# Order of the q and oT low parts, of the first layer norms and of the first head tiles in an adaLN attention and gated FFN block

## The chip, the cores and the metric

The kernel runs on one core of a Trainium2 chip. The metric is the device time of one execution in microseconds (us). The engines are named as the profile names them: PE (matrix engine, with PEld for its weight loads), DVE (vector engine), ACT (scalar engine), POOL (GpSimd) and SP, whose queue issues the DMAs and the transposing DMAs.

## The reference

One block of a transformer with adaptive layer norm, all in float32. The shapes: 2048 rows of 512, 32 heads of 128, attention over the last 512 rows of the key and value caches, a feed-forward width of 1376.

```python
mod = (silu(c) @ w_mod).reshape(1, 6, 1, 512)
sa, ca, ga, sb, cb, gb = (mod[:, i] for i in range(6))
h = layernorm(x) * (1 + ca) + sa
# attention: q = h @ wq, per head over the last W = 512 rows of the caches
scores = q @ k.T * 128 ** -0.5
x = x + ga * ((softmax(scores) @ v) @ wo)
h = layernorm(x) * (1 + cb) + sb
x = x + gb * ((gelu(h @ w_gate) * (h @ w_up)) @ w_down)
```

## The kernel before

Each float32 operand of a large matmul is held as a pair of float16 tiles, a high part (a scaled cast) and a low part (the scaled operand less its high part). A product takes three matmuls: high by high, high by low, low by high. The casts are made on ACT, the low parts on DVE (`scalar_tensor_tensor`) or on POOL (a subtraction).

The attention runs over 128 iterations: 16 groups of two heads; in a group, four groups of 512 queries; for each of these, the two heads in turn. One iteration does q = h @ wq for 512 queries (`q_proj`, 12 matmuls of 128x128 by 512 columns into the one PSUM bank psQ), the scores (`s_mm`, 12, in two halves of 256 queries, each into a pair of banks psS of which there are two), the softmax (`s_max` on DVE, `s_exp` on ACT, `s_low` on POOL and the transposing DMAs), probabilities by v (`pv`, 12, into the one bank psO) and the product with wo (`wo_mm`, 12, two banks psW), which DVE adds to the accumulator `acc` (`wo_add`).

The order is written out by hand. `slot(i)` emits one turn: the scores of iteration i, the product with v of iteration i - 2, the product with wo of i - 3 (its first quarter for i - 2), the q projection of i + 2, and the high and low part of q for i + 1 (`q_high` on ACT, L303; `q_low` on DVE, L306) and of the attention output oT for i - 2 (`o_high` on ACT, L368; `o_low` on DVE, L371). Every engine executes its own instructions in the order in which they were emitted, and waits where an operand or a buffer isn't ready.

In `s_max` (L323, L325) DVE takes the maxima of a half's two score rows in one reduction over 128x1024 and makes the exponent's bias of each in an operation on 128x1. `s_exp` (L334, L337) makes two exponentials with their sums and a cast of both to float16. `s_low` (L342) subtracts on POOL and issues two transposing DMAs.

Everything else is hung between as background work: `at(half, f, ...)` puts a call into a list, and `hooks(half)` in `slot` empties the list at that place. A slot has six such places, in this order: 2i + 0.25 (behind the first half's scores), 2i + 0.5, 2i (the end of the first half), 2i + 1.25 (behind the second half's scores), 2i + 1.5, 2i + 1 (the end of the slot). Calls at one place keep the order in which they were put in.

Background work is, in the first slots, the layer norms of the query groups 1 to 3 (`ln_stats`, `ln_norm`, and `ln1_chunk`, which transposes a chunk on PE and makes the pair hh, hl) and the tiles of v and wo of the first two heads (`h_max`, `h_cross_a` and `h_cross_b` for their common scale over all partitions, `h_scalars`, `h_quick`). Later it is loading, scaling and splitting of the next two heads (`load_raw`, `h_max`, `h_scale` on POOL, L272, `h_split` on ACT and POOL, L277 and L278, `h_turn`), the rest of the modulation (`mod_mul`, L559 and L561), the maxima of the feed-forward weights, and in the last slots the first weights of the feed-forward and the second layer norm of the first 512 rows (`ln2_norm`, `ln2_chunk`, `ln2_high`, `ln2_low`). Raw tiles live in eight buffers; a load waits for the last reader of its buffer.

`ln_norm` on ACT needs a factor (L136, on DVE) for a group of four rows, which it makes when first called; on POOL it takes two operations (L139, L140), on DVE one (L142).

The feed-forward follows the last slot: 44 units of 24 matmuls, the activation, and 12 matmuls with w_down.

Of the kernel before, what the change touches and what calls it, by code (L numbers as in the profile page):

```python
# [11 lines left out]
AF = mybir.ActivationFunctionType  # L12
OP = mybir.AluOpType
# [28 lines left out]
def adaln_block(ctx: ExitStack, tc: tile.TileContext, x, k_cache, v_cache, wq, wo,  # L42
                w_gate, w_up, w_down, c_in, w_mod, out):
    nc = tc.nc
# [6 lines left out]
    base = ctx.enter_context(tc.tile_pool(name="base", bufs=1, side="left"))  # L51
# [7 lines left out]
    def small(pool, cols_, bufs=3, name="sm"):  # L59
        return pool.tile([P, cols_], F32, name=name, tag=name, bufs=bufs)  # L60
# [5 lines left out]
    acc = [base.tile([P, D], F32, name=f"acc{t}", tag=f"acc{t}") for t in range(SQ // P)]  # L66
# [10 lines left out]
    mxs = [base.tile([P, P], F32, name=f"mx{i}", tag=f"mx{i}") for i in range(3)]  # L77
# [36 lines left out]
    MV, RS, LNP, LNF = {}, {}, {}, {}  # L114
# [13 lines left out]

    NMR = {}

    def ln_norm(key, dst, src, j, eng=None):
        rs = RS[key][:, j:j + 1]
        if eng is nc.scalar:
            if key not in NMR:
                NMR[key] = small(base, 4, 2, "nmr")
                nc.vector.scalar_tensor_tensor(NMR[key], MV[key][:, :, 0], -1.0, RS[key], op0=OP.mult, op1=OP.mult)  # L136
            nc.scalar.activation(dst, src, AF.Identity, scale=rs, bias=NMR[key][:, j:j + 1])
        elif eng is nc.gpsimd:
            nc.gpsimd.tensor_scalar(dst, src, MV[key][:, j, 0:1], 1.0, op0=OP.subtract, op1=OP.mult)  # L139
            nc.gpsimd.tensor_scalar(dst, dst, rs, 1.0, op0=OP.mult, op1=OP.mult)  # L140
        else:
            nc.vector.tensor_scalar(dst, src, MV[key][:, j, 0:1], rs, op0=OP.subtract, op1=OP.mult)  # L142
# [35 lines left out]
    RAW = {}  # L178
# [39 lines left out]
    HW, DG, IV, AV, ES, RV = {}, {}, {}, {}, {}, {}  # L218
# [17 lines left out]
    def h_scalars(h, part=None):  # L236
        if h not in ES:
            ES[h] = small(base, 2, 5, "es")
            RV[h] = ES[h][:, 1:2]
        if part in (None, "qk"):  # L240
            nc.vector.scalar_tensor_tensor(ES[h][:, 0:1], IV.pop(("wq", h)), sc1[:, 1:2], IV.pop(("k", h)),
                                           op0=OP.mult, op1=OP.mult)
        if part in (None, "vo"):
            nc.vector.scalar_tensor_tensor(ES[h][:, 1:2], IV.pop(("v", h)), 1.0 / ODOWN, IV.pop(("wo", h)),
                                           op0=OP.mult, op1=OP.mult)
# [4 lines left out]
    def h_tile(kind, h):  # L250
        t = right.tile([P, 2, N], F16, name=kind, tag=kind, bufs=BUFS[kind]) if kind != "k" else \
            right.tile([P, 2, N], F16, name="k16", tag="k16", bufs=2)
        (K16 if kind == "k" else HW)[kind, h] = t
        return t

    def h_turn(kind, h):
        t = K16.pop((kind, h))
        kt = HW[kind, h] = right.tile([P, 2, N], F16, name="kT", tag="kT", bufs=BUFS[kind])
        nc.sync.dma_start_transpose(kt.rearrange("p a (b k) -> p (a b) k", b=4), t.rearrange("p a b -> p (a b)"))

    def h_quick(kind, h):
        raw, a = RAW.pop((kind, h)), AV[kind, h]
        t = h_tile(kind, h)
        nc.scalar.activation(t[:, 0, :], raw, AF.Copy, scale=a)
        nc.vector.scalar_tensor_tensor(t[:, 1, :], raw, a, t[:, 0, :], op0=OP.mult, op1=OP.subtract)  # L265
        if kind == "k":
            h_turn(kind, h)


    def h_scale(kind, h):  # L270
# [3 lines left out]
    def h_split(kind, h):  # L274
        raw = RAW.pop((kind, h))
        t = h_tile(kind, h)
        nc.scalar.activation(t[:, 0, :], raw, AF.Copy)  # L277
        nc.gpsimd.tensor_tensor(t[:, 1, :], raw, t[:, 0, :], op=OP.subtract)  # L278
# [26 lines left out]
    def q_low(it):  # L305
        nc.vector.scalar_tensor_tensor(Q[it][:, 1, :], PSQ.pop(it), QDOWN, Q[it][:, 0, :],  # L306
                                       op0=OP.mult, op1=OP.subtract)
# [94 lines left out]
    def ln1_split(qg, c, full, low):  # L402
        pt = LNP.pop((qg, c))
        f = right.tile([P, N], F32, name="h32", tag="h32", bufs=2)
        a, b = colA[1][:, c:c + 1], colB[1][:, c:c + 1]
        if full is nc.scalar:
            nc.scalar.activation(f, pt, AF.Identity, scale=a, bias=b)
            nc.scalar.activation(hh[qg][:, c, :], f, AF.Copy)
        else:
            nc.scalar.activation(hh[qg][:, c, :], pt, AF.Identity, scale=a, bias=b)  # L410
            nc.vector.tensor_scalar(f, pt, a, b, op0=OP.mult, op1=OP.add)
        low.tensor_tensor(hl[qg][:, c, :], f, hh[qg][:, c, :], op=OP.subtract)  # L412
# [4 lines left out]
    V, S_, Y = nc.vector, nc.scalar, nc.gpsimd  # L417
# [3 lines left out]
    for j in range(4):  # L421
        ln_norm(0, acc[j], acc[j], j, S_)
# [5 lines left out]
    for j in (1, 0):  # L428
# [4 lines left out]
        for f in range(NC):  # L433
            n = 4 * (1 - j) + f
# [8 lines left out]
    later = [(kind, h) for h in range(G) for kind in ("v", "wo")]  # L443
# [16 lines left out]
    nc.vector.tensor_scalar_mul(cols[:, 0:8], cols[:, 0:8], sc1[:, 0:1])  # L460
    h_scale("k", 0)
    ln1_split(0, 0, V, V)
    h_quick("wq", 0)
    ln1_split(0, 1, V, V)
    h_split("k", 0)
    h_turn("k", 0)
# [11 lines left out]
    h_cross_b(second, two[:, 1, :])  # L478
    h_scale("k", 1)
    h_scalars(1, "qk")  # L480
    h_quick("wq", 1)
    h_split("k", 1)
    h_turn("k", 1)
    for j in (2, 3):
# [5 lines left out]
    def at(half, f, *a):  # L490
        bg.setdefault(half, []).append((f, a))

    def hooks(half):
        for f, a in bg.pop(half, []):
            f(*a)
# [7 lines left out]
    for j in range(4):  # L503
        at(0.5, ln_norm, 1, acc[4 + j], acc[4 + j], j)
    for c, (tag, full, low) in enumerate((("psW", V, V), ("psW", S_, Y), ("psO", V, V), ("psW", S_, Y))):
        at(1.5, ln1_chunk, 1, c, tag, full, low)
    for j in range(4):
        at(1, ln_stats, 2, acc[8 + j], j)
    for i, kh in enumerate(later):
        at(1, h_max, kh, mxs[2], i)  # L510
    at(1, h_cross_a, later, mxs[2])
    at(2.25, h_cross_b, later)
    for h in range(G):
        at(2.25, h_scalars, h, "vo")
        at(2 + 2 * h, h_quick, "v", h)
        at(3 + 2 * h, h_quick, "wo", h)
    for j in range(4):
        at(2, ln_norm, 2, acc[8 + j], acc[8 + j], j, S_ if j % 2 else Y)
        at(2 + j // 2, ln_stats, 3, acc[12 + j], j)
        at(4, ln_norm, 3, acc[12 + j], acc[12 + j], j, S_ if j % 2 else Y)  # L520
    for c, (half, full, low) in enumerate(((3.5, V, V), (3.5, S_, Y), (4.25, V, V), (4.25, S_, Y))):
        at(half, ln1_chunk, 2, c, "psW", full, low)
# [4 lines left out]
    for g in range(1, NG):  # L527
        b = 2 * PER * (g - 1)
        for n, (dl, dm, dc, dsp) in enumerate(((-3, 0, 5, 8), (2, 5, 9, 12))):
            h = g * G + n  # L530
# [109 lines left out]
    def slot(i):  # L640
        def when(it, f, *a):
            if 0 <= it < NIT:
                f(it, *a)

        when(i, s_mm, 0)
        hooks(2 * i + 0.25)
        when(i - 3, wo_add, 0)
        when(i + 1, q_high)
        when(i - 3, wo_mm, 1)
        when(i, s_max, 0)  # L650
        hooks(2 * i + 0.5)
        when(i, s_exp, 0)
        when(i + 1, q_low)
        when(i, s_low, 0)
        when(i - 2, pv, 0, 2)
        when(i - 3, wo_mm, 2)
        when(i - 3, wo_add, 1)
        when(i - 2, pv, 2, 4)
        hooks(2 * i)

        when(i, s_mm, 1)
        hooks(2 * i + 1.25)
        when(i - 2, o_high)
        when(i - 3, wo_add, 2)
        when(i, s_max, 1)
        hooks(2 * i + 1.5)
        when(i + 2, q_proj, 0, 2)
        when(i, s_exp, 1)
        when(i - 2, o_low)
        when(i, s_low, 1)  # L670
        when(i - 3, wo_mm, 3)
        when(i + 2, q_proj, 2, 4)
        when(i - 2, wo_mm, 0)
        when(i - 3, wo_add, 3)
        when(i - 2, s_rec)
        hooks(2 * i + 1)
# [172 lines left out]
    for j in range(4):  # L849
        at(e + 4, x1_load, 0, j)  # L850
        n = e + 8 + (j + 1) // 2
# [4 lines left out]
    for f in range(NDA):  # L856
        at(e + 6, wd_load, f)
        at(e + 11 + f, ff_scale, "d", f)
        at(e + 12 + f, ff_part, "d", f)
    for c, (a, b) in enumerate(((13.5, 13), (13, 14.5), (14.5, 14), (14, 15.5))):  # L860
        at(e + a, ln2_chunk, 0, c, nc.vector if c % 2 else nc.scalar)
        at(e + a, ln2_high, 0, c)
        at(e + b, ln2_low, 0, c, nc.gpsimd)
# [10 lines left out]
    for i in range(NIT + 3):  # L874
        slot(i)
# [3 lines left out]
    while nd < NU:  # L879
# [5 lines left out]
        if u < NU:  # L885
# [23 lines left out]
            if qg + 1 < NQG and f >= 7:  # L909
                c = f - 7  # L910
# [34 lines left out]
```

## Time and profile before

| | us |
|---|---|
| median of three runs | 1802.39 |
| lowest and highest | 1801.22, 1802.88 |
| the profiled execution | 1801.44 |
| its span, first to last instruction | 1799.6 |
| PE busy in it | 1738.2 |
| DVE, ACT, POOL busy | 1311.0, 1010.9, 862.6 |

The profiled execution has a time of its own, 1.8 us above its span; sums over stretches of the trace are made against it. A row of a group or of the timeline names the line of the kernel, the engine, the operation, the tile written and the tiles read; the arrow in brackets behind a row names what ended the engine's idle time ahead of it. Operations of one engine overlap a little in their records, so the price of one in a row of others is the distance of two starts.

### The profile page before, as it was taken

The numbers are of one execution on the slowest core, as the hardware profiler recorded it, in microseconds if no ns is written. First come the engines' busy times: TensorE is split into PE (matmuls) and PEld (weight loads), VectorE is DVE, ScalarE is ACT, GpSimd is POOL, SyncE is SP. The second block draws the span as 40 slices with busy tenths as digits, with TensorE's granted clock in tenths as the row PEclk, the third lists the DMA queues.
The fourth block names the chain that finished last, engine by engine and source line by source line (L and its number), as shares of the span: only waits on it lengthen the run. The fifth ranks groups of instructions, "written<-read, shape, count | busy, mean of one in ns | idle before, by whom it ended". The sixth has DMA issues, their size and how long they took to land.

```text
span 1799.6 us, 23663 instructions
## 1 busy us (share of the span) xinstructions
PE 1738.2 (97%) x8106; PEld 807.5 (45%) x8106; DVE 1311.0 (73%) x2468; ACT 1010.9 (56%) x1866; POOL 862.6 (48%) x606
## 2 busy tenths in 40 slices
PE   7599999999999999999999999999999899999998
PEld 5244444444444444444444444444444344444443
DVE  7687878887888888888888888888987756424222
ACT  3567676666667575766566666657576534121211
POOL 2546665665646474746565555646377600101010
PEclk8799999999999999999999999999999999999999
DMA  6358686867677776868786868687668521101000
GB/s 199 76 97 162 129 171 105 181 115 161 125 154 141 139 149 129 152 127 151 138 167 114 170 116 165 131 149 132 125 130 153 118 87 43 48 1 47 1 24 24
DMA packets 658952, 213.54 MB, mean 119 GB/s; under 512 B 580304, under 2 KB 640720, under 8 KB 658832
## 3 DMA queue, kind: packets, MB, share of 16 engines
q1 hardware_dynamic: 658832, 212.03, 59.5%
q8 instruction: 64, 1.05, 0.2%
q14 instruction: 56, 0.46, 0.1%
HBM read 65.14 MB, written 4.19 MB: 39 GB/s over the span
## 4 chain that ended last, share of the span: by engine, by line
PE 85%; DVE 9%; POOL 2%; ACT 2%; issue 2%; DMA 0%; SPq 0%; DVEq 0%; POOLq 0%; ACTq 0%
PE psW L378 6%; PE psQ L297 6%; PE psQ L299 6%; PE psQ L298 6%; PE psW L380 5%; PE psW L379 5%; PE psS L315 5%; PE psS L317 5%; PE psS L316 5%; PE psO L362 5%; PE psO L363 5%; PE psO L364 5%; PE psS L796 4%; PE psS L797 4%; PE psS L798 4%
## 5 line engine op out<-in xcount | busy, mean ns | idle before, releaser
L342 POOL TENSOR_TENSOR pp<-p,pp 128x1024 f16<-128x1024 f32 x256 | 544.8, 2128 | 561.1 <-ACT pp L337 528.1
L334 ACT ACTIVATE p<-psS,st,es 128x512 f32<-128x512 f32 x512 | 393.3, 772 | 448.3 <-DVE st L325 435.7
L323 DVE TENSOR_REDUCE st<-psS 128x2 f32<-128x1024 f32 x256 | 312.5, 1221 | 143.4 <-PE psS L317 141.9
L390 DVE SCALAR_TENSOR_TENSOR acc<-psW,st,acc 128x512 f32<-128x512 f32 x496 | 364.4, 743 | 23.7 <-PE psW L380 19.7
L337 ACT ACTIVATE pp<-p 128x1024 f16<-128x1024 f32 x256 | 270.6, 1057 | 8.1
L378 PE MATMUL psW<-wo,oT 128*128 128x512 f16 x512 | 195.0, 381 | 15.9 <-DVE acc L390 10.6
L297 PE MATMUL psQ<-hh,wq 128*128 128x512 f16 x512 | 196.1, 383 | 5.6 <-DVE q L306 2.0
L380 PE MATMUL psW<-wo,oT 128*128 128x512 f16 x512 | 195.0, 381 | 3.5 <-DVE oT L371 3.5
L298 PE MATMUL psQ<-hl,wq 128*128 128x512 f16 x512 | 195.7, 382 | 2.7 <-DVE hl L412 1.6
L315 PE MATMUL psS<-kT,q 128*128 128x512 f16 x512 | 196.5, 384 | 0.3 <-DMA kT<-k 0.3
L316 PE MATMUL psS<-kT,q 128*128 128x512 f16 x512 | 196.5, 384 | 0.0
L317 PE MATMUL psS<-kT,q 128*128 128x512 f16 x512 | 196.5, 384 | 0.0
L299 PE MATMUL psQ<-hh,wq 128*128 128x512 f16 x512 | 196.0, 383 | 0.3 <-DVE wq L265 0.3
L379 PE MATMUL psW<-wo,oT 128*128 128x512 f16 x512 | 195.2, 381 | 0.0
L364 PE MATMUL psO<-pT,v 128*128 128x512 f16 x512 | 194.3, 380 | 0.0
L363 PE MATMUL psO<-pT,v 128*128 128x512 f16 x512 | 194.3, 379 | 0.0
L362 PE MATMUL psO<-pT,v 128*128 128x512 f16 x512 | 194.3, 379 | 0.0
L805 DVE SCALAR_TENSOR_TENSOR gl<-psS,ffs,gl 128x512 f32<-128x512 f32 (+1 forms) x44 | 33.0, 750 | 178.5 <-ACT gl L804 178.5
L804 ACT ACTIVATE gl<-psS,ffs 128x512 f32<-128x512 f32 (+1 forms) x44 | 30.2, 687 | 219.9 <-PE psS L798 219.9
L334 ACT ACTIVATION_READ_ACCUMULATOR p<-psS,st,es 128x1 f32 x512 | 99.2, 194 | 0.0
L325 DVE TENSOR_SCALAR st<-st,es 128x1 f32<-128x1 f32 x512 | 85.6, 209 | 9.1
L371 DVE SCALAR_TENSOR_TENSOR oT<-psO,oT 128x512 f16<-128x512 f32 x128 | 87.2, 682 | 6.1 <-ACT oT L368 5.5
(219 smaller groups left out, 2670.5 us busy)
## 6 DMA issues: line engine op xcount, KB each, us to landing
raw<-in_A_wq_dram SPq DMA_DIRECT2D x32, 256.0 KB, 3.3
raw<-in_A_k_cache_dram SPq DMA_DIRECT2D x32, 256.0 KB, 3.6
raw<-in_A_v_cache_dram SPq DMA_DIRECT2D x32, 256.0 KB, 4.6
raw<-in_A_wo_dram SPq DMA_DIRECT2D x32, 256.0 KB, 4.9
pT<-pp SPq DMA_TRANSPOSE x512, 3.2
raw<-in_B_w_down_dram SPq DMA_DIRECT2D x20, 256.0 KB, 2.9
raw<-in_B_w_gate_dram SPq DMA_DIRECT2D x18, 256.0 KB, 3.5
raw<-in_B_w_up_dram SPq DMA_DIRECT2D x18, 256.0 KB, 3.6
```

Source lines behind the costliest of these rows:

```text
L297: nc.tensor.matmul(pq, wh, hh[qg][:, c, :], start=(c == 0), stop=False)
L298: nc.tensor.matmul(pq, wh, hl[qg][:, c, :], start=False, stop=False)
L299: nc.tensor.matmul(pq, w[:, 1, c * P:(c + 1) * P], hh[qg][:, c, :], start=False, stop=(c == NC - 1))
L315: nc.tensor.matmul(p[:, j, :], q[:, 0, qs], k[:, 0, :], start=True, stop=False)
L316: nc.tensor.matmul(p[:, j, :], q[:, 0, qs], k[:, 1, :], start=False, stop=False)
L317: nc.tensor.matmul(p[:, j, :], q[:, 1, qs], k[:, 0, :], start=False, stop=True)
L323: nc.vector.tensor_reduce(st[:, 2 * b:2 * b + 2], PSS[it, b], op=OP.max, axis=AX.X, negate=True)
L334: nc.scalar.activation(p32[:, j, :], p[:, j, :], AF.Exp, bias=st[:, n:n + 1], scale=ES[head_qg(it)[0]][:, 0:1], accum_out=st[:, 4 + n:5 + n])
L342: nc.gpsimd.tensor_tensor(pp[:, :, 1, :], p32, pp[:, :, 0, :], op=OP.subtract)
L378: nc.tensor.matmul(p, o[:, 0, ts], w[:, 0, :], start=True, stop=False)
L379: nc.tensor.matmul(p, o[:, 0, ts], w[:, 1, :], start=False, stop=False)
L390: nc.vector.scalar_tensor_tensor(a, p, r, a, op0=OP.mult, op1=OP.add)
```

## The change

Five things are reordered; the arithmetic stays.

1. In a slot's first half DVE makes the low part of q for i + 1 ahead of the maxima of that half's scores, where it stood behind the maxima. In slot 0 it stays behind them.
2. In the second half DVE makes the low part of oT for i - 2 ahead of the maxima, where it stood behind them.
3. `h_quick` is split into `h_high` (ACT) and `h_low` (DVE). For v and wo of the first two heads the high parts stay at their places, and the low parts come at 3.25, 4.25, 5.25 and 6.25.
4. The norm of query group 2 goes from place 2 to 2.25, the first part of the common scale of v and wo from 1 to 2.25 and its second part from 2.25 to 2; the factor for group 3's norm is made at 4.25.
5. Each chunk of the second layer norm ahead of the feed-forward moves one place later.

```diff
+    def ln_nmr(key):
+        NMR[key] = small(base, 4, 2, "nmr")
+        nc.vector.scalar_tensor_tensor(NMR[key], MV[key][:, :, 0], -1.0, RS[key], op0=OP.mult, op1=OP.mult)
+
     def ln_norm(key, dst, src, j, eng=None):
...
-    def h_quick(kind, h):
-        raw, a = RAW.pop((kind, h)), AV[kind, h]
+
+    def h_high(kind, h):
         t = h_tile(kind, h)
-        nc.scalar.activation(t[:, 0, :], raw, AF.Copy, scale=a)
-        nc.vector.scalar_tensor_tensor(t[:, 1, :], raw, a, t[:, 0, :], op0=OP.mult, op1=OP.subtract)
-        if kind == "k":
-            h_turn(kind, h)
+        nc.scalar.activation(t[:, 0, :], RAW[kind, h], AF.Copy, scale=AV[kind, h])
+
+    def h_low(kind, h):
+        t = HW[kind, h]
+        nc.vector.scalar_tensor_tensor(t[:, 1, :], RAW.pop((kind, h)), AV[kind, h], t[:, 0, :],
+                                       op0=OP.mult, op1=OP.subtract)
...
     for j in range(4):
         at(1, ln_stats, 2, acc[8 + j], j)
+        at(2.25, ln_norm, 2, acc[8 + j], acc[8 + j], j, S_ if j % 2 else Y)
+        at(2 + j // 2, ln_stats, 3, acc[12 + j], j)
     for i, kh in enumerate(later):
         at(1, h_max, kh, mxs[2], i)
-    at(1, h_cross_a, later, mxs[2])
-    at(2.25, h_cross_b, later)
+    at(2.25, h_cross_a, later, mxs[2])
+    at(2, h_cross_b, later)
     for h in range(G):
-        at(2.25, h_scalars, h, "vo")
-        at(2 + 2 * h, h_quick, "v", h)
-        at(3 + 2 * h, h_quick, "wo", h)
+        at(2, h_scalars, h, "vo")
+        for n, kind in enumerate(("v", "wo")):
+            at(2 + 2 * h + n, h_high, kind, h)
+            at(3.25 + 2 * h + n, h_low, kind, h)
+    at(4.25, ln_nmr, 3)
     for j in range(4):
-        at(2, ln_norm, 2, acc[8 + j], acc[8 + j], j, S_ if j % 2 else Y)
-        at(2 + j // 2, ln_stats, 3, acc[12 + j], j)
         at(4, ln_norm, 3, acc[12 + j], acc[12 + j], j, S_ if j % 2 else Y)
...
         when(i - 3, wo_mm, 1)
+        if i:
+            when(i + 1, q_low)
         when(i, s_max, 0)
         hooks(2 * i + 0.5)
+        if i == 0:
+            q_low(1)
         when(i, s_exp, 0)
-        when(i + 1, q_low)
         when(i, s_low, 0)
...
         when(i - 3, wo_add, 2)
+        when(i - 2, o_low)
         when(i, s_max, 1)
         hooks(2 * i + 1.5)
         when(i + 2, q_proj, 0, 2)
         when(i, s_exp, 1)
-        when(i - 2, o_low)
         when(i, s_low, 1)
...
-    for c, (a, b) in enumerate(((13.5, 13), (13, 14.5), (14.5, 14), (14, 15.5))):
+    for c, (a, b) in enumerate(((13, 14.5), (14.5, 14), (14, 15.5), (15.5, 15))):
```

More of the change, by code (lines that the diff above doesn't have):

```diff
@@ L134, in ln_norm @@
             if key not in NMR:
-                NMR[key] = small(base, 4, 2, "nmr")
-                nc.vector.scalar_tensor_tensor(NMR[key], MV[key][:, :, 0], -1.0, RS[key], op0=OP.mult, op1=OP.mult)
+                ln_nmr(key)
             nc.scalar.activation(dst, src, AF.Identity, scale=rs, bias=NMR[key][:, j:j + 1])
@@ L462, in adaln_block @@
     ln1_split(0, 0, V, V)
-    h_quick("wq", 0)
+    h_high("wq", 0)
+    h_low("wq", 0)
     ln1_split(0, 1, V, V)
@@ L480, in adaln_block @@
     h_scalars(1, "qk")
-    h_quick("wq", 1)
+    h_high("wq", 1)
+    h_low("wq", 1)
     h_split("k", 1)
```

## The prediction

> I read the page first, then the stretches between the starts of slots 0, 8 and 120 (a slot is one turn of the hand-written order, one head against one group of 512 queries), then single slots instruction by instruction on each engine, then the waits of the two ends.
>
> **What bounds it now.** The page's share of busy time, and the three stretches (columns: from:to, length, then busy us of PE, its weight loads, DVE, ACT and POOL with counts, the granted clock, DMA share, GB/s):
>
> ```profile
> PE 1738.2 (97%) x8106; PEld 807.5 (45%) x8106; DVE 1311.0 (73%) x2468; ACT 1010.9 (56%) x1866; POOL 862.6 (48%) x606
> 34.34:152.94 118.60, 92.24 (x398) 42.77 (x398) 89.48 (x170) 71.72 (x129) 67.04 (x50) 0.86 0.46 89
> 152.94:1340.98 1188.04, 1176.09 (x5484) 538.31 (x5483) 991.81 (x1909) 778.77 (x1473) 692.24 (x462) 1.00 0.75 142
> 1340.98:1452.00 111.02, 102.46 (x464) 46.13 (x463) 78.08 (x141) 63.54 (x117) 69.27 (x50) 0.97 0.65 129
> ```
>
> The middle stretch holds 112 slots of 10.61 us, with PE busy 99% of it at full clock: PE sets the pace there. In the first and last stretch it has holes. A slot without extra work, by the first score matmuls of slots 16 and 17:
>
> ```profile
> 238.23 0.38 PE L315 MATMUL psS<-kT,q 128*128 128x512 f16 x1
> ...
> 248.59 0.38 PE L315 MATMUL psS<-kT,q 128*128 128x512 f16 x1
> ```
>
> That is 10.36 us for 48 matmuls. DVE and ACT are partly idle, but share of idle time doesn't tell whether an order of work is free: ACT and DVE hand each other the maxima, exponentials and casts, and the change rewrites just those hand-overs.
>
> **Low parts ahead of the maxima.** No instruction and no DMA is added in a slot; slot 0 alone keeps q's old place. Today DVE does the maximum (L323, L325) and then the low part (L306 or L371), so a low part may wait for its cast on ACT (L303, L368) while ACT is already fed with the next exponential. Afterwards DVE stands at the low part until ACT has made the cast, with the maximum queued behind it; ACT, in order too, makes the cast only after the exponentials of the half before; and those need the maximum of the half before. So each half becomes one chain: maximum, exponentials, cast, low part, next maximum. It closes on itself over the two halves of a slot, and DVE and ACT no longer overlap on it. Its four links, from rows. DVE:
>
> ```profile
> 244.90 1.22 DVE L323 TENSOR_REDUCE st<-psS 128x2 f32<-128x1024 f32 x1 [1.08 <-PE psS L317]
> 246.16 0.33 DVE L325 TENSOR_SCALAR st<-st,es 128x1 f32<-128x1 f32 x2
> 246.41 0.68 DVE L371 SCALAR_TENSOR_TENSOR oT<-psO,oT 128x512 f16<-128x512 f32 x1
> 247.01 0.74 DVE L390 SCALAR_TENSOR_TENSOR acc<-psW,st,acc 128x512 f32<-128x512 f32 x1
> 247.67 0.17 DVE L351 RECIPROCAL st<-st 128x4 f32<-128x4 f32 x1
> ```
>
> ACT in the same half:
>
> ```profile
> 246.47 0.78 ACT L334 ACTIVATE p<-psS,st,es 128x512 f32<-128x512 f32 x1 [0.85 <-DVE st L325]
> ...
> 249.10 0.58 ACT L303 ACTIVATE q<-psQ 128x512 f16<-128x512 f32 x1
> ```
>
> And one cast for which a low part did wait, on ACT and then on DVE:
>
> ```profile
> 267.26 0.58 ACT L368 ACTIVATE oT<-psO 128x512 f16<-128x512 f32 x1
> 267.87 0.69 DVE L371 SCALAR_TENSOR_TENSOR oT<-psO,oT 128x512 f16<-128x512 f32 x1 [0.65 <-ACT oT L368]
> ```
>
> Maximum to exponential 244.90 to 246.47, 1.57; exponential to cast 246.47 to 249.10, 2.63; cast to low part 267.26 to 267.87, 0.61; low part to the next DVE work 246.41 to 247.01, 0.60. The half is 5.41, the slot **10.82 us** against PE's 10.36. What ACT does between exponential and cast lengthens the chain as well, since ACT is in order and idle only behind the cast. That is above all the high half of the next heads' tiles, L277; its price is the distance of two starts:
>
> ```profile
> 718.05 0.61 ACT L277 ACTIVATE wq<-raw 128x512 f16<-128x512 f32 x1
> 718.58 0.58 ACT L303 ACTIVATE q<-psQ 128x512 f16<-128x512 f32 x1
> ```
>
> 0.53 us, and in the middle stretch there are 4 times 28 of them and 12 modulation rows (L561), 0.10 longer each, which I put at 0.63:
>
> ```profile
> L277 ACT ACTIVATE v<-raw x28: 612/613/630, 154.0 to 1320.4; 128x512 f16<-128x512 f32 x28
> L277 ACT ACTIVATE wo<-raw x28: 612/613/615, 158.6 to 1327.5; 128x512 f16<-128x512 f32 x28
> L277 ACT ACTIVATE wq<-raw x28: 612/614/631, 206.0 to 1331.7; 128x512 f16<-128x512 f32 x28
> L277 ACT ACTIVATE k<-raw x28: 612/613/630, 211.3 to 1336.3; 128x512 f16<-128x512 f32 x28
> ```
>
> ```profile
> L561 ACT ACTIVATE raw<-raw,silu 128x512 f32<-128x512 f32 x12 | 8.5, 710 | 5.5 <-DMA raw<-in_w_mod_dram 5.5
> ```
>
> Stretch after: 112 x 10.82 + 112 x 0.53 + 12 x 0.63 = 1211.8 + 59.4 + 7.6 = 1278.8, less 1188.04: **+91**. A second way, from ACT's idle time:
>
> ```profile
> L334 ACT ACTIVATE p<-psS,st,es 128x512 f32<-128x512 f32 x448 | 344.2, 772 | 393.9 <-DVE st L325 390.1 <-POOL pp L342 1.8 <-PE psW L380 1.7
> ```
>
> ACT idles 393.9 / 224 = 1.76 us ahead of each half's exponentials; in the closed chain it is 0.61 - 0.58 + 0.60 + 1.57 = 2.20, so 224 x 0.44 = +99. The two agree within 8; I keep 91. The links scatter by some 0.05 a half in the slots I looked at, 11 us over 224 halves, either way. The remaining DVE work is no part of this sum: from the start of the second maximum to the q low part DVE has 1.57 + 2.63 + 0.61 = 4.81 us, and in it stand 1.51 for maximum and constants (244.90 to 246.41), two additions of 0.66 (247.01 to 247.67) and the reciprocal, about 3.2 in all. That cover gone is a rival below. PE's own extra holes in a slot (its waits for L390) are inside the longer slot. PE waits once in a slot instead, at L380 for the o low part, and is some 3 us ahead of DVE everywhere else: a half slot of matmuls is 5.18, the chain's 5.41. POOL, SP and the transposes keep their order in the slot and get more time.
>
> **First slots.** The waits of PE and of DVE from 30 us on (us in total, times, longest), and POOL there:
>
> ```profile
> PE psW L147 <- POOL acc L140: 10.3, 2, 8.2
> PE psW L378 <- ACT oT L368: 4.1, 1, 4.1
> PE psO L97 <- DVE mx L226: 3.0, 1, 3.0
> ```
>
> ```profile
> DVE v L265 <- ACT v L264: 5.4, 2, 2.7
> DVE wo L265 <- ACT wo L264: 5.4, 2, 3.2
> ```
>
> ```profile
> 53.27 1.02 POOL L126 TENSOR_TENSOR rs<-ve,eps_t 128x4 f32<-128x4 f32 x1
> 61.12 2.12 POOL L342 TENSOR_TENSOR pp<-p,pp 128x1024 f16<-128x1024 f32 x1 [6.84 <-ACT pp L337]
> 63.22 2.44 POOL L139 TENSOR_SCALAR acc<-acc,mv 128x512 f32<-128x512 f32 x1
> ```
>
> The norms of query group 2 move ahead of slot 1's first subtraction (L342): they can start at 54.3 instead of 63.2, so of PE's 8.2 us I take away 6; the score matmuls of slot 1 now run ahead of the transpose L97, which waits for the maxima of v and wo, 3 more. The cross-maximum's second part, the scalars and the group 3 statistics change places inside slot 1 without an added instruction. Lows of v and wo come one and a quarter or so halves behind their highs, which frees DVE of 10.8 us of waits; from slot 2 on the closed chain paces DVE anyway, so I count 3. The raw buffers come free as much later, and the next heads' loads, on SP ahead of later transposes, wait for them; each low still stands on DVE ahead of its load, so nothing. The early statistics factor of group 3 (L136) takes a wait of ACT out, inside the same chain. Against it slots 5 to 7 have the longer chain and seven copies: 3 x 0.46 + 7 x 0.53 = 5. Sum -6 - 3 - 3 + 5 = **-7**. Bounds: all waits gain in full, -24 (10.3 + 3.0 + 10.8); nothing gains, +5. The value lies between, nearer the walk through slot 1, the one place where I see what is late next.
>
> **End.** The layer norm 2 chunks come one place later, so that the transposes no longer stand waiting for the norms:
>
> ```profile
> PE psQ L147 <- DVE raw L142: 2.9, 2, 1.9
> ```
>
> At most -2.9, at worst nothing. The chain adds 7 x 0.46 and eight weight copies at 0.53, 7.5. Together **+5**, bounds +1 and +12.
>
> **Sum.** The profiled execution took 1801.44 us, 1.8 beyond its span and 0.95 under the median 1802.39, inside the three runs' 1801.22 to 1802.88. 1801.4 + 91 - 7 + 5 = **1890**.
>
> **Rivals.** 1. *DVE's side work falls inside the chain.* The scalars of a new head, now and then, stand still for as long as POOL subtracts. POOL, then DVE:
>
> ```profile
> 705.64 2.13 POOL L342 TENSOR_TENSOR pp<-p,pp 128x1024 f16<-128x1024 f32 x1 [2.64 <-ACT pp L337]
> 705.68 2.10 DVE L244 SCALAR_TENSOR_TENSOR es<-iv 128x1 f32<-128x1 f32 x1
> ```
>
> With 2.1 for it and two raw maxima of about 0.7 the 3.2 becomes 6.7 against 4.81: 1.9 twice per pair of heads, 14 pairs, +53 at most; half of that, +26, **1916**. Against: in the chain POOL starts at the cast and is done before DVE gets to the scalars.
>
> 2. *The copies hide.* If ACT had time for the copies off the chain, the stretch would take 1211.8, +24 only, and the ends, without their copies too, some -11 and +1: **1815**. For: ACT still idles 2.2 us in each half. Against: that idle time lies behind the cast, and the copies stand ahead of it.
>
> 3. *Not slower.* If ACT finishes its casts before the score matmuls are in, the low part fits into DVE's own wait (1.08 in the row of 244.90), the chain never closes, PE keeps 10.36 and only the gains at the ends stay: -12 and -3, **1786**. It decides at a half of 5.18 with the copies in it; mine is 5.41 and 5.94. An order that DVE didn't follow would give the same 1802 as now, but the rows above stand in program order.
>
> 4. *PE's clock falls.* PE would stand idle up to 1.5 us in each slot. Gaps like that were harmless so far, a long one wasn't:
>
> ```profile
> 1280.52 0.38 PE L378 MATMUL psW<-wo,oT 128*128 128x512 f16 x1 [2.07 <-DVE acc L390]
> ```
>
> ```profile
> 53.32 0.63 PE L315 MATMUL psS<-kT,q 128*128 128x512 f16 x1
> 53.75 0.63 PE L316 MATMUL psS<-kT,q 128*128 128x512 f16 x1
> ```
>
> After the 3.0 us wait for L226, matmuls start 0.43 apart, not 10.36 / 48 = 0.216. Ten of them so in each slot are 2.1 us, PE's slot 12.5 against the chain's 11.4: 112 x 1.1 = +123, **2013**. The Trainium skill speaks for this rival (TensorE: Matmul & The Clock Gate, "A second HAM failure mode: psum-queue depth-cycling"): frequent short idling between groups of matmuls can make the clock gate swing. By that rule the time would be the 2013; the trace has single gaps of 2 us without it, and none that recurs every slot.
>
> **Chances.** The closed chain, 1890: 0.73, own range 1868 to 1912 (the links' 11 and half the ends' bounds). Rival 1: 0.13. Rival 2: 0.04. Rival 3: 0.06, most of it faster. Rival 4: 0.04. The range 1862 to 1920 takes in rival 1. A measurement here tells 0.2%, 3.6 us, from no change: faster 0.05, same 0.01, slower 0.94.
>
> **What would show it.** Right: in a free slot the score matmuls are about 10.8 apart, in loaded ones up to 11.9; L306 and L371 stand ahead of L323 and idle for ACT's casts; ACT waits some 2.2 for L325 in every half; PE's busy share of the stretch falls to 92%; PE's waits name L371 at L380. Wrong: L323 still idles for PE's scores, or free slots stay at 10.4.

## The result

The changed kernel takes 1912.78 us (median of four runs, 1908.96 to 1916.7) against 1801.81 of the kernel before (1799.49 to 1802.88). The ratio is 1.0618, 95% interval 1.059 to 1.0645: slower. Its profiled execution took 1916.7 us with a span of 1914.8, so the trace shows 115 us more than that of before, 4 of them above the median.

In the changed kernel the lines moved: L306 is L311 (q's low part), L303 is L308 (its cast), L323 and L325 are L328 and L330 (maxima), L334 is L339 (exponentials), L342 is L347 (POOL's subtraction), L368 and L371 are L373 and L376 (oT's cast and low part), L378 and L380 are L383 and L385, L390 is L395, L277 is L282, L241 and L244 are L244 and L247.

From the page of the kernel before: the chain of work that ended last, by engine, and the groups of exponentials and maxima.

```profile
PE 85%; DVE 9%; POOL 2%; ACT 2%; issue 2%; DMA 0%; SPq 0%; DVEq 0%; POOLq 0%; ACTq 0%
...
L334 ACT ACTIVATE p<-psS,st,es 128x512 f32<-128x512 f32 x512 | 393.3, 772 | 448.3 <-DVE st L325 435.7
L323 DVE TENSOR_REDUCE st<-psS 128x2 f32<-128x1024 f32 x256 | 312.5, 1221 | 143.4 <-PE psS L317 141.9
```

The page of the change: busy shares, the same chain, and the groups of exponentials, maxima and low parts.

```profile
PE 1785.6 (93%) x8106; PEld 799.9 (42%) x8106; DVE 1249.7 (65%) x2468; ACT 1010.2 (53%) x1866; POOL 861.3 (45%) x606
...
ACT 35%; DVE 28%; PE 22%; issue 9%; POOL 3%; DMA 1%; SPq 1%; ACTq 0%; POOLq 0%; DVEq 0%
...
L339 ACT ACTIVATE p<-psS,st,es 128x512 f32<-128x512 f32 x512 | 393.3, 772 | 579.2 <-DVE st L330 577.0
...
L328 DVE TENSOR_REDUCE st<-psS 128x2 f32<-128x1024 f32 x256 | 310.7, 1214 | 2.4 <-PE psS L322 2.3
...
L376 DVE SCALAR_TENSOR_TENSOR oT<-psO,oT 128x512 f16<-128x512 f32 x128 | 88.5, 691 | 231.3 <-ACT oT L373 231.3
...
L311 DVE SCALAR_TENSOR_TENSOR q<-psQ,q 128x512 f16<-128x512 f32 x128 | 88.4, 690 | 142.1 <-ACT q L308 142.0
```

The reader is to see that none of these groups takes longer to execute by more than 10 ns an operation, and that the waits changed places: the maxima, which stood 142 us waiting for PE's scores, wait 2.3 us; the low parts wait 373 us for ACT's casts; ACT waits 577 us for the maxima in place of 436. The last chain, which was 85% PE, is 35% ACT and 28% DVE. No engine is busy more than 93%: the time is set by two engines that wait for each other.

A slot without copies on ACT, slot 65 of the change, on DVE:

```profile
823.16 1.21 DVE L328 TENSOR_REDUCE st<-psS 128x2 f32<-128x1024 f32 x1
824.41 0.34 DVE L330 TENSOR_SCALAR st<-st,es 128x1 f32<-128x1 f32 x2
...
827.98 0.69 DVE L376 SCALAR_TENSOR_TENSOR oT<-psO,oT 128x512 f16<-128x512 f32 x1 [1.32 <-ACT oT L373]
828.59 1.21 DVE L328 TENSOR_REDUCE st<-psS 128x2 f32<-128x1024 f32 x1
...
833.40 0.69 DVE L311 SCALAR_TENSOR_TENSOR q<-psQ,q 128x512 f16<-128x512 f32 x1 [0.97 <-ACT q L308]
834.01 1.21 DVE L328 TENSOR_REDUCE st<-psS 128x2 f32<-128x1024 f32 x1
```

And on ACT:

```profile
824.75 0.78 ACT L339 ACTIVATE p<-psS,st,es 128x512 f32<-128x512 f32 x1 [2.22 <-DVE st L330]
...
827.37 0.58 ACT L373 ACTIVATE oT<-psO 128x512 f16<-128x512 f32 x1
830.16 0.78 ACT L339 ACTIVATE p<-psS,st,es 128x512 f32<-128x512 f32 x1 [2.22 <-DVE st L330]
...
832.79 0.58 ACT L308 ACTIVATE q<-psQ 128x512 f16<-128x512 f32 x1
```

Followed from row to row across the two engines this is one closed line: maxima 823.16, exponentials 824.75, cast 827.37, low part 827.98, maxima 828.59, exponentials 830.16, cast 832.79, low part 833.40, maxima 834.01. The slot takes 10.85 us, and every link starts as soon as the one before allows.

Where the time came from, by starts of DVE's first maxima in slots 8 and 120 (from:to, length, busy us of PE, its weight loads, DVE, ACT, POOL, granted clock, DMA share, GB/s); first the kernel before, then the change:

```profile
154.43:1342.48 1188.05, 1176.10 (x5484) 538.31 (x5483) 991.44 (x1909) 779.24 (x1474) 691.56 (x461) 1.00 0.75 141
1342.48:1799.60 457.12, 442.11 (x2059) 205.26 (x2057) 206.87 (x339) 149.28 (x250) 97.19 (x76) 0.99 0.23 57
```

```profile
155.43:1453.68 1298.25, 1221.23 (x5484) 532.43 (x5483) 936.93 (x1909) 778.35 (x1472) 690.67 (x461) 0.99 0.67 129
1453.68:1914.80 461.12, 440.37 (x2043) 202.13 (x2041) 203.45 (x339) 149.08 (x249) 96.24 (x76) 0.99 0.23 55
```

Up to slot 8 the change is 1.0 us longer, the middle stretch 110.2, the rest 4.0. In the middle PE does the same 5484 matmuls and is busy 94% of the time; ACT is as busy as before. The 1912.8 lies 0.8 above the prediction's own range of 1868 to 1912 and inside its wider one of 1862 to 1920, which took in the first rival's 1916.

### The profile page after: what moved, and what is told of

Same layout as the page of the kernel before. It is cut to its first block, busy times and chain, and to the rows that moved or that the text cites. A ratio compares the mean times of both kernels' runs of the same rounds, so it can differ in the third digit from the quotient of the medians.

```text
span 1914.8 us, 23669 instructions
## 1 busy us (share of the span) xinstructions
PE 1785.6 (93%) x8106; PEld 799.9 (42%) x8106; DVE 1249.7 (65%) x2468; ACT 1010.2 (53%) x1866; POOL 861.3 (45%) x606
## 4 chain that ended last, share of the span: by engine, by line
ACT 35%; DVE 28%; PE 22%; issue 9%; POOL 3%; DMA 1%; SPq 1%; ACTq 0%; POOLq 0%; DVEq 0%
DVE st L328 14%; ACT p L339 13%; ACT pp L342 12%; DVE oT L376 4%; DVE q L311 4%; PE psS L809 4%; PE psS L810 4%; PE psS L808 4%; DVE st L330 3%; ACT oT L373 3%; ACT q L308 3%; POOL pp L347 1%; PE psW L831 1%; PE psW L832 1%; PE psW L833 1%
## 5 line engine op out<-in xcount | busy, mean ns | idle before, releaser
L347 POOL TENSOR_TENSOR pp<-p,pp 128x1024 f16<-128x1024 f32 x256 | 544.6, 2127 | 686.3 <-ACT pp L342 622.4
L339 ACT ACTIVATE p<-psS,st,es 128x512 f32<-128x512 f32 x512 | 393.3, 772 | 579.2 <-DVE st L330 577.0
L395 DVE SCALAR_TENSOR_TENSOR acc<-psW,st,acc 128x512 f32<-128x512 f32 x496 | 364.3, 742 | 15.1 <-PE psW L385 11.4
L328 DVE TENSOR_REDUCE st<-psS 128x2 f32<-128x1024 f32 x256 | 310.7, 1214 | 2.4 <-PE psS L322 2.3
L342 ACT ACTIVATE pp<-p 128x1024 f16<-128x1024 f32 x256 | 270.5, 1057 | 8.1
L383 PE MATMUL psW<-wo,oT 128*128 128x512 f16 x512 | 195.5, 382 | 68.8 <-DVE acc L395 39.3
L376 DVE SCALAR_TENSOR_TENSOR oT<-psO,oT 128x512 f16<-128x512 f32 x128 | 88.5, 691 | 231.3 <-ACT oT L373 231.3
L385 PE MATMUL psW<-wo,oT 128*128 128x512 f16 x512 | 195.6, 382 | 8.0 <-DVE oT L376 0.2
L303 PE MATMUL psQ<-hl,wq 128*128 128x512 f16 x512 | 196.4, 384 | 2.7 <-DVE hl L417 1.6
L368 PE MATMUL psO<-pT,v 128*128 128x512 f16 x512 | 195.4, 382 | 0.0
L311 DVE SCALAR_TENSOR_TENSOR q<-psQ,q 128x512 f16<-128x512 f32 x128 | 88.4, 690 | 142.1 <-ACT q L308 142.0
L339 ACT ACTIVATION_READ_ACCUMULATOR p<-psS,st,es 128x1 f32 x512 | 99.1, 194 | 0.0
```

The lines of the kernel that those rows point to most:

```text
L303: nc.tensor.matmul(pq, wh, hl[qg][:, c, :], start=False, stop=False)
L328: nc.vector.tensor_reduce(st[:, 2 * b:2 * b + 2], PSS[it, b], op=OP.max, axis=AX.X, negate=True)
L339: nc.scalar.activation(p32[:, j, :], p[:, j, :], AF.Exp, bias=st[:, n:n + 1], scale=ES[head_qg(it)[0]][:, 0:1], accum_out=st[:, 4 + n:5 + n])
L342: nc.scalar.activation(pp[:, :, 0, :], p32, AF.Copy)
L347: nc.gpsimd.tensor_tensor(pp[:, :, 1, :], p32, pp[:, :, 0, :], op=OP.subtract)
L395: nc.vector.scalar_tensor_tensor(a, p, r, a, op0=OP.mult, op1=OP.add)
```

## The experiments

Two theories were put against each other first. **Closed chain:** the loss needs both moves, since either alone leaves a chain shorter than PE's slot. **Each move by itself:** every low part that waits for its cast holds up DVE, so each move costs its share. Then the chain was made shorter and longer, and PE was given less to do.

The table gives, for the profiled execution of each kernel, where slot 8's first maxima start, the length from there to slot 120's, and the rest to the end of the span; then the median of the timed runs and the ratio to the kernel before on the same chip. The stretches are of one execution each; the timed runs of one kernel lie up to 7 us apart, so a few microseconds in one stretch are weak evidence.

| kernel | to slot 8 | slots 8 to 119 | rest | median us | ratio (95%) |
|---|---|---|---|---|---|
| before | 154.4 | 1188.1 | 457.1 | 1801.8 | |
| the change | 155.4 | 1298.3 | 461.1 | 1912.8 | 1.0618 (1.059 to 1.0645) |
| q's low part first | 150.9 | 1188.9 | 455.4 | 1799.1 | 0.9987 (0.9978 to 0.9996) |
| oT's low part first | 145.0 | 1180.4 | 458.7 | 1789.9 | 0.9934 (0.9917 to 0.995) |
| staging alone | 145.9 | 1188.9 | 460.4 | 1797.6 | 0.9978 (0.997 to 0.9987) |
| both orders alone | 163.5 | 1294.5 | 462.3 | 1924.9 | 1.0694 (1.0674 to 1.0714) |
| oT first, old chunks | 144.8 | 1180.3 | 461.2 | 1790.0 | 0.9936 (0.9924 to 0.9949) |
| copies behind the cast | 151.0 | 1234.6 | 460.6 | 1850.2 | 1.0270 (1.0256 to 1.0284) |
| change, cast twice | 159.9 | 1365.7 | 464.3 | 1988.8 | 1.1036 (1.102 to 1.1053) |
| before, cast twice | 153.0 | 1188.9 | 457.1 | 1802.4 | 1.0005 (0.9996 to 1.0014) |
| fewer matmuls | 158.3 | 1296.1 | 461.2 | 1914.4 | 1.0636 (1.0617 to 1.0656) |
| before, oT first | 154.1 | 1181.7 | 461.1 | 1799.1 | 0.9996 (0.9987 to 1.0005) |
| before, scalars later | 154.3 | 1176.4 | 456.3 | 1789.4 | 0.9940 (0.9927 to 0.9952) |
| staging, scalars later | 146.2 | 1176.2 | 456.3 | 1783.1 | 0.9905 (0.9887 to 0.9922) |

### One move alone

q's low part first, against the change:

```diff
         when(i - 3, wo_add, 2)
-        when(i - 2, o_low)
         when(i, s_max, 1)
...
         when(i, s_exp, 1)
+        when(i - 2, o_low)
```

> The change with oT's low part back behind the maxima of the second half; q's low part stays ahead of those of the first half. Closed chain: the chain needs both moves. With oT's low part out of it, the slot's chain is maxima to exponentials 1.57, to the oT cast 2.62, the cast 0.50, the second exponentials 2.62, to q's low part 0.61, to the maxima 0.61, in all 8.5, or 9.6 with two copies, under the 10.36 us of PE. So PE sets the pace again, only the gains of the first and last slots stay: about 1793. Each move costs by itself (rival): the cost is shared as DVE's waits for the casts are (142.0 us at L311, 231.3 at L376, profile of the change), so q alone keeps some 46 of 120: about 1839.

oT's low part first, against the change:

```diff
-        if i:
-            when(i + 1, q_low)
         when(i, s_max, 0)
         hooks(2 * i + 0.5)
-        if i == 0:
-            q_low(1)
         when(i, s_exp, 0)
+        when(i + 1, q_low)
```

> The change with q's low part back behind the maxima of the first half; oT's low part stays ahead of those of the second half. Closed chain: open again, as with q alone, about 1793, slots without extra work 10.36 us apart. Each move costs by itself (rival): oT alone keeps some 74 of 120: about 1867.

Measured: 1799.1 and 1789.9. The middle stretch takes 1188.9 and 1180.4 us, against 1188.1 before. The rival's 1839 and 1867 are out: neither move costs anything there alone, and together they cost 110. ACT's wait ahead of the exponentials with q's low part first, from the groups of its middle stretch, is that of before, 388.9 / 224 = 1.74 us a half:

```profile
L339 ACT ACTIVATE p<-psS,st,es 128x512 f32<-128x512 f32 x448 | 344.0, 772 | 388.9 <-DVE st L330 379.6 <-PE psW L385 9.1
```

Two things were not as expected. q first missed 1793 by 6. It reaches slot 8 5 us later than the staging alone (150.9 against 145.9), but is 5 us shorter after slot 120, and the staging alone misses 1793 by 5 as well. oT first is 8.4 us better in the middle than the staging alone; that is taken up below.

### The staging alone, and the orders alone

The staging alone has both edits shown above; the orders alone are the kernel before with only these lines changed:

```diff
+        if i:
+            when(i + 1, q_low)
         when(i, s_max, 0)
         hooks(2 * i + 0.5)
+        if i == 0:
+            q_low(1)
         when(i, s_exp, 0)
-        when(i + 1, q_low)
...
+        when(i - 2, o_low)
         when(i, s_max, 1)
...
         when(i, s_exp, 1)
-        when(i - 2, o_low)
```

> The change with both low parts back behind the maxima: only the staging of the first slots and the later layer norm chunks are left. Closed chain: the staging saves what the first slots of the changed kernel show before the chain has eaten it (6 us at the first maximum of slot 2) and up to 3 at the end: about 1793. Rival, the staging itself is a part of the loss (the third slot of the changed kernel is 19.9 us long from maximum to maximum): 1802 or more.

> The kernel before with both low parts ahead of the maxima and nothing else of the change. Closed chain: the middle stretch as in the change, +110, the first slots without the staging some 6 us longer and the end some 2: about 1920. Rival, the loss comes in part from the staging: clearly under 1913.

Measured: 1797.6 and 1924.9, each 5 us above what was expected. The staging is no part of the loss: it saves 8.5 us to slot 8 where the chain isn't closed (145.9 against 154.4) and 8.1 where it is (155.4 against 163.5). At the end the staging run is 3.3 us longer than before, so that only 3 to 4 us of the gain are left in its time.

### The chain made shorter

The high halves of the next heads' tiles (L282) are put where ACT waits anyway, behind the cast and ahead of the next exponentials. Their low halves on POOL (L283), which are no link of the chain, move with them:

```diff
-                at(b + dsp + i + 1, h_split, kind, h)
+                at(b + dsp + i + 2.5, h_split, kind, h)
```

> The change with the ACT copies of the next heads' tiles put one and a half places later, so that on ACT they come behind the cast and ahead of the next exponentials, where ACT waits 2.2 us for the maxima. Closed chain: 112 copies of 0.53 leave the chain of the middle stretch and the rest of 120 that of the last slots, loaded slots go from 11.8 to 10.8: -63, about 1850. Rival, the loss isn't a chain over ACT but DVE work or contention: within 10 of 1913.

Measured: 1850.2, the expected 1850. On ACT, in a loaded slot of the change, the copy stands between the exponentials and the cast and ACT then waits 2.20 us:

```profile
871.23 0.61 ACT L282 ACTIVATE k<-raw 128x512 f16<-128x512 f32 x1
871.75 0.58 ACT L373 ACTIVATE oT<-psO 128x512 f16<-128x512 f32 x1
874.52 0.78 ACT L339 ACTIVATE p<-psS,st,es 128x512 f32<-128x512 f32 x1 [2.20 <-DVE st L330]
```

In the experiment it stands in that wait, which is 1.68 us long:

```profile
859.14 0.58 ACT L308 ACTIVATE q<-psQ 128x512 f16<-128x512 f32 x1
859.62 0.62 ACT L282 ACTIVATE v<-raw 128x512 f16<-128x512 f32 x1
861.92 0.78 ACT L339 ACTIVATE p<-psS,st,es 128x512 f32<-128x512 f32 x1 [1.68 <-DVE st L330]
```

The same work on the same engine costs half a microsecond or nothing, by its place in the chain. In the change a slot with none, one or two copies takes 10.84, 11.36 and 11.84 us (medians of slots 8 to 119 without modulation work); with the copies moved it takes 10.85, 10.85 and 10.80. In sum 1298.3 - 1234.6 = 63.7 us for 112 copies, 0.57 each.

### The chain made longer, and the same work off it

In the change and in the kernel before, q's cast is made twice:

```diff
         nc.scalar.activation(Q[it][:, 0, :], PSQ[it], AF.Copy, scale=QDOWN)
+        nc.scalar.activation(Q[it][:, 0, :], PSQ[it], AF.Copy, scale=QDOWN)
```

> The change with q's cast on ACT made twice. Closed chain: each second cast stands in the chain and costs its distance of starts, 0.48 (105.53 to 106.01 on ACT in the profile before), 126 times: +60, about 1973. Rival, PE or the transposes set the pace: within 5 of 1913, since ACT is busy only 53% of the span.

> The kernel before with q's cast on ACT made twice. Closed chain: before, there is no chain through ACT and DVE that is longer than PE's slot, the second cast falls into the 1.76 us that ACT idles in each half: within 5 of 1801. Rival, ACT's time counts in both orders: +60, about 1861.

Measured: +76 (1988.8) and nothing (1802.4). The sign and the contrast are the closed chain's; the size is a quarter more than expected. The second cast (L309), into the same tile, starts when the first has ended, 0.61 after it and not 0.48, and the low part 0.63 after that:

```profile
1560.69 0.58 ACT L308 ACTIVATE q<-psQ 128x512 f16<-128x512 f32 x1
1561.30 0.60 ACT L309 ACTIVATE q<-psQ 128x512 f16<-128x512 f32 x1
```

```profile
1561.93 0.69 DVE L312 SCALAR_TENSOR_TENSOR q<-psQ,q 128x512 f16<-128x512 f32 x1 [2.49 <-ACT q L309]
```

From the first cast to the low part that is 1.24 in place of 0.61, 0.63 more; 126 such slots would make 79 us, and 76 were measured.

### Less work for PE

```diff
-            nc.tensor.matmul(pq, wh, hl[qg][:, c, :], start=False, stop=False)
```

> The change with 44 matmuls in an attention slot in place of 48: the product of the layer norm's low part with wq is left out, so the result is another. Closed chain: PE isn't what the slots wait for, the middle stretch stays at 1298 us and the whole within 8 of 1913. Rival, PE still sets the pace in the change: 512 matmuls of 0.216 less, -110, about 1803.

Measured: 1914.4. With 448 matmuls fewer in the middle stretch the stretch is as long, 1296.1 us; PE is busy 88% of it. PE doesn't set the time of the changed kernel:

```profile
158.30:1454.40 1296.10, 1145.63 (x5036) 481.39 (x5035) 934.76 (x1909) 778.72 (x1472) 690.75 (x461) 0.99 0.68 129
```

### What oT's low part gains, and a version that beats both

With oT first DVE is busy 937.2 us in the middle stretch and not 993.2. Of the 56 us, 50 are the scalars of each new head (L244 and L247, 128x1 each), which before the change meet POOL's subtraction and then last as long as it does (the pair of rows in the prediction's first rival). Their groups in the middle stretch, before:

```profile
L241 DVE SCALAR_TENSOR_TENSOR es<-iv,sc 128x1 f32<-128x1 f32 x28 | 30.0, 1072 | 0.0
L244 DVE SCALAR_TENSOR_TENSOR es<-iv 128x1 f32<-128x1 f32 x28 | 27.3, 976 | 0.1
```

In the run with oT first, none of the two is longer than 0.22 us, and PE's waits for the accumulators fall from 9.4 to 2.9 us in the middle. First the staging alone, then oT first:

```profile
PE psW L383 <- DVE acc L395: 9.4, 12, 2.1
```

```profile
PE psW L383 <- DVE acc L395: 2.9, 3, 2.2
```

Whether it is the order that gains or only the meeting that it avoids was asked with two edits of the kernel before: oT's low part first and nothing else, and the old order with the scalars moved.

```diff
         when(i - 3, wo_add, 2)
+        when(i - 2, o_low)
         when(i, s_max, 1)
...
         when(i, s_exp, 1)
-        when(i - 2, o_low)
```

> The kernel before with oT's low part ahead of the maxima of the second half and nothing else. The middle stretch of the run with the staging and oT first took 1180.4 us against 1188.9 with the staging alone; in it DVE's scalars of a new head (L244, L247) no longer meet POOL's subtraction and PE waits 2.9 in place of 9.4 for L395. If that gain is the order's alone: -8, about 1793. Rival, it needs the staging: 1801.

```diff
-            at(b + dc + 2, h_scalars, h)
+            at(b + dc + 3.5, h_scalars, h)
```

> The kernel before with the scalars of each new head one and a half places later, behind the maxima of the next first half, when POOL is done with its subtraction; both low parts where they were. If the 8 us are DVE standing still in those scalars while POOL subtracts: -8 as with oT first, about 1793. Rival, oT's low part gains in another way: 1801.

Measured: 1799.1, no difference that can be told, and 1789.4. oT first gains 6.4 us in the middle and gives 4.0 back after slot 120. The scalars later gain 11.6 in the middle and lose nothing; L241 and L244 fall to 13.5 and 4.2 us there, their longest to 0.87. With oT first they fall further, to 4.7 and 4.3, and yet the middle gains 5 less. So the gain is the meeting avoided; the order of oT's low part was one way to avoid it and gains nothing of its own here.

Then the two gains together, the staging without the later chunks and the scalars later, against the change:

```diff
-        if i:
-            when(i + 1, q_low)
...
-        if i == 0:
-            q_low(1)
...
+        when(i + 1, q_low)
...
-        when(i - 2, o_low)
...
+        when(i - 2, o_low)
...
-            at(b + dc + 2, h_scalars, h)
+            at(b + dc + 3.5, h_scalars, h)
...
-    for c, (a, b) in enumerate(((13, 14.5), (14.5, 14), (14, 15.5), (15.5, 15))):
+    for c, (a, b) in enumerate(((13.5, 13), (13, 14.5), (14.5, 14), (14, 15.5))):
```

> The kernel before with the first slots staged as in the change, the scalars of each new head one and a half places later, and nothing else: both low parts behind the maxima, the second layer norm's chunks at their old places. If the two gains are of separate places they add up: -8.5 for the first slots (first maximum of slot 8 at 145.9 in the staging run against 154.4) and -11.7 for the middle stretch (1176.4 in the run with the scalars later against 1188.05): about 1781. Rival, they overlap, or the end takes back 3 as in the staging run: 1785 to 1790.

Measured: 1783.1, ratio 0.9905 (0.9887 to 0.9922). The gains add up, to slot 8 and in the middle stretch within 0.3 us of what each run showed alone. It beats the kernel before by 18 us and the change by 130; 1781 was expected. PE is busy 1172.1 of 1176.2 us in its middle stretch:

```profile
146.20:1322.40 1176.20, 1172.13 (x5484) 537.91 (x5483) 947.56 (x1909) 778.39 (x1474) 691.67 (x461) 1.00 0.75 143
```

### The later layer norm chunks

> The change with q's low part back behind the maxima, and with the second layer norm's chunks at the places they had before. The staging run was 3.3 us longer than before from the first maximum of slot 120 to its end (460.4 against 457.1). If that is the later chunks, this is some 3 under the run with oT's low part first (1789.9): about 1787. Rival, the later chunks gain as forecast and something else takes 3 there: 1790 or more.

The edit is the one in the last diff's last two lines, made in the run with oT's low part first. Measured: 1790.0 against 1789.9, no difference. The expected 3 us aren't there; in this pair the old places are 2.5 us longer after slot 120 (461.2 against 458.7), while the staging run with the later chunks was 3.3 longer than before. What sets the few us of the end stays open.

## Why the prediction was right, and where its sizes were off

The forecast, slower by a chain closed over DVE and ACT, stands: one move alone costs nothing in the middle, both cost 110, a copy taken out of the chain gives its half microsecond back, and work added to it costs in full. The size was less good: 88 us were forecast and 111 came, which lies closer to rival 1's 1916 than to 1890, and half of what the middle stretch missed is rival 1's mechanism in another place.

- **The links.** 1.57, 2.63, 0.61, 0.60 were forecast; over slots 8 to 119 of the change the starts give 1.57, 2.62, 0.61 and 0.61 where nothing else stands between. A free slot was to take 10.82 and takes 10.84.
- **The copies.** 0.53 each in the chain: near enough, since the run that takes them out gains 0.57 each.
- **The middle stretch, forecast +91, measured +110.** This is the term that was mis-sized. Its base, 1211.8, is right. Work and waits of ACT between exponentials and cast took 73.8 us in place of 67.0: four first modulation rows (L559 before), left out of the sum, some 2.5, and the waits of ACT for a DMA (2.6) and for PE (1.8) in the same stretch. And DVE reached low parts and maxima late by 13 us, which the prediction had put at nothing. Nearly all of it is in five slots. In three of them, 9.5 us together, an operation of DVE lasts as long as POOL's subtraction and stands ahead of a low part: a scalar of a new head in slot 35, and two operations for the feed-forward scales, the second with a dozen small ones behind it, in slots 112 and 113. Here the cross-maximum of slot 112 waits for PE and then stands 2.08 us, ahead of q's low part; behind it the other two:

```profile
1366.08 0.29 DVE L99 TENSOR_REDUCE mr<-psO 128x1 f32<-128x128 f32 x1 [0.57 <-PE psO L97]
1366.40 2.08 DVE L101 TENSOR_SCALAR dg<-ident,mr 128x8 f32<-128x8 f32 x1
1368.40 0.74 DVE L395 SCALAR_TENSOR_TENSOR acc<-psW,st,acc 128x512 f32<-128x512 f32 x1
1369.06 0.67 DVE L311 SCALAR_TENSOR_TENSOR q<-psQ,q 128x512 f16<-128x512 f32 x1
```

```profile
489.02 2.09 DVE L247 SCALAR_TENSOR_TENSOR es<-iv 128x1 f32<-128x1 f32 x1
...
1379.80 2.08 DVE L630 COPY ffs<-av 128x3 f32<-128x3 f32 x1
```

In the other two, slots 27 and 34, 3.6 us together, DVE waits for PE around a row of the modulation, and then the maxima wait 1.2 us for scores that PE makes at half its clock (rival 4 below).

- **Rival 1** named that mechanism, but for the scalars of each head, where it was to be +26 and is about 3: in the chain POOL is done before DVE gets there, as was argued against it, and one of the 56 scalars of the middle stretch still met a subtraction (489.02 above). With the two operations for the feed-forward scales the mechanism comes to 9.5 us, which the prediction had put at nothing.
- **The first slots, forecast -7, measured +1.** The staging was to gain 12 and gains 8.5; the chain was to take 5 there and takes 9.5 (155.4 against 145.9). Slots 5 to 7 were counted for it; the run with q first shows 5 us of loss without a closed chain in these eight slots, so part of it seems to be q's low part alone; that the norms and first tiles on ACT are the reason was not tried.
- **The end, forecast +5, measured +4.** The chunks' part of it, at most -2.9, can't be told from nothing.
- **Rival 2**, copies that hide: they don't where they stand; they do once moved, which is the experiment's 1850.
- **Rival 3**, not slower: its deciding point was a half of 5.18 with the copies in it. It holds for either move alone.
- **Rival 4**, a falling clock: it didn't fall in every slot, and the granted clock of the middle stretch is 0.99, but it fell four times. The Trainium skill's rule (TensorE: Matmul & The Clock Gate, "A second HAM failure mode: psum-queue depth-cycling") had PE's clock swing with frequent short idling; here PE waits at L383 in most slots, up to 2.0 us in the middle stretch, and the clock doesn't swing with them. It stood at 0.50 for 3.4 to 6.8 us behind four of PE's longest waits there, of 1.9 to 3.1 us; two waits at L575, of 2.0 and 2.2 us, had no fall behind them. The first fall, at slot 27 (a window of the change, with the columns of the stretches above):

```profile
391.00:395.30 4.30, 4.30 (x11) 1.51 (x10) 3.10 (x6) 0.98 (x3) 1.09 (x1) 0.50 0.48 90
```

In the chain the falls show as the 2.3 us that two maxima waited for scores. The prediction's row of 2.07 us without a fall is no safe bound: a wait of 2.02 us at 1384.5 had one behind it.

- **The signs.** Four of five were right: free slots (the score matmuls 10.93 apart in the median), the low parts' place and idle time, ACT's wait (508 us / 224 = 2.27) and, nearly, PE's share, 94% and not 92. PE's wait was to show at L385 for oT's low part; it shows at L383, the first matmul of the same product, for the accumulators' bank and for oT's cast. In the middle of the change:

```profile
PE psW L383 <- DVE acc L395: 28.0, 71, 2.0
PE psW L383 <- ACT oT L373: 23.5, 49, 1.3
```

## What to carry to other kernels

Ahead of moving an operation of one in-order engine in front of another, follow the waits in a ring through both engines and add the links: if the ring closes within one turn of the loop and its sum is longer than the bounding engine's turn, the difference is paid in every turn, though both engines are half idle and each move alone is free. What stands in such a ring is worth moving to where the engine waits. A tiny operation that lasts as long as another engine's large one is a meeting, and a place half a turn later can be worth more than the reordering that it was found by.

## What was not expected of the hardware

Of the 56 scalars of new heads (L241 and L244, 128x1) in the middle stretch of the kernel before, 25 lasted until POOL's subtraction ended, nearly all of them 2.1 us; the others took 0.14 to 0.17. The Trainium skill (SBUF — State Buffer, "SBUF: two separate sides") has DVE and GpSimd take one shared pair of ports in turn for the length of an instruction, when the DVE operation has two inputs in SBUF or runs in a two-port mode; L244 of the kernel before, which reads two tiles, agrees, 2.10 against 0.15. The biases of the exponentials (L325 before), also 128x1 and with POOL at work under most of them, last 0.20 to 0.22 in all cases. They read one tile and a scalar where L244 reads two tiles; no run here tries whether that is what sets them apart. That moving those scalars gains 11.6 us, of some 48 us in which DVE stood still in them (57.3 less 28 times 0.17 and 28 times 0.15), was shown; that PE's waits for the accumulators are the way by which it does was read from the two rows above (with the scalars later they fall from 8.7 to 2.1 us) and not tried by itself.
